# V's matmuls ahead of P's transposes in three of a unit's five slots

## The chip, the cores and the metric

The kernel runs on one core of one Trainium2 chip. The metric is device time in microseconds (us) of one execution; the times shown are medians of several runs. The engines are named as the profile names them: PE (TensorE's matmuls), PEld (its weight loads), DVE (VectorE), ACT (ScalarE), POOL (GpSimd) and SP (which issues the transfers).

## The reference

An attention with a learned bias, then a feed-forward layer whose gate is a cosine. In numpy, for q, k, v of 4 batches, 8 heads, 576 positions and 64 channels:

```
scores = q @ k.T / 8 + bias[head]          # bias from log positions through a small MLP
attn   = softmax(scores)                   # over the 576 keys
x      = (attn @ v) laid out as 2304 x 512 # tokens x model width
h      = x @ w_in                          # 512 -> 2048
out    = (h * cos(h)) @ w_out              # 2048 -> 512
```

## The kernel before

A first stage makes the bias table, a second the attention, a third the feed-forward layer. The change is in the second.

**Units and slots.** A unit is one pair of heads of one batch; there are 16 (`NU`), u = 0 to 15. A unit has five slots, j = 0 to 4, one for each block of queries: `tiles = [0, 1, 4, 2, 3]`, so the slots with j = 0, 1, 3, 4 have 128 queries of both heads, and j = 2 has the last 64 queries of both heads together. The text calls them first to fifth slot. The whole order of work is written by hand: `slot(i)` issues the instructions of slot i, and each engine runs its own instructions in exactly that order.

**What one slot issues on PE.** First the scores of this slot (`qk`, L416), 12 matmuls into two PSUM buffers (`ps_s`), one for each head; in the third slot 6. Then `halves` (L477, here called flips), which transposes by matmul the probabilities P of the block three slots earlier (`prev`) into two PSUM buffers `pm`, tags `m0` and `m1`, of which there is one each. Then `pv` (L545), V's matmuls, a part of the previous unit's output: `PV_EARLY` gives the first slot chunks 0 and 1 and the second slot chunks 2 to 4 of half 0, the fourth slot chunks 0 to 2 and the fifth chunks 3 and 4 of half 1; the third slot has none. A half sums up in one PSUM buffer (`ps_v`), of which there is one, so chunk 0 of a half has to wait until the half before has been copied away.

**The second slot** of units 1 to 13 already has `pv` ahead of `halves` (`v_first`); the copies of its flips are put off to the third slot (`held`). There, ahead of the scores, PE also transposes the q and k of unit u + 2 (`spare`).

**What the other engines issue.** In the order of each queue in a slot:

- DVE: for each head, scores plus bias and their extremum (L429), which also frees the head's score buffer; a copy of the flips in `m1` out of PSUM (`keep_main` with r = 1, L508); sums and reciprocals (L460, L463); in some slots one step that widens a weight (L101 to L107).
- ACT: the exponentials of the slot before, one for each head (`softmax_exp`, L447); a copy of the flips in `m0` (`keep_main` with r = 0, L505, tile PT); in the first and fourth slots a copy of leftover flips (`keep_left`, L505, tile PX), in the first also two of a q piece (L223); `keep_x` (L505, tile xT), which copies a finished half out of `ps_v`, in the third slot (half 0) and in the fifth (half 1). In the third slot, ACT has the exponentials, then the copy held over from the second slot, then a copy of q (L212, tile qt), then `keep_x`, then its own copy of the flips. In the fifth slot of odd units two weight operations stand in the queue: L93 ahead of the copy of the flips, L109 between it and `keep_x`.
- POOL: the splits of q and k (L185, L189) and the normalising of P (L470).

The copies of the flips fill PT, which `pv` reads later: the copies of a unit's flips of half 0 end in its fifth slot and are first read in the next unit's first slot; those of half 1 end in the third slot of the next unit and are first read in its fourth.

Of the kernel before, what the change touches and what calls it, by code (L numbers as in the profile page):

```python
# [28 lines left out]
def kernel(  # L29
# [44 lines left out]
    NU = len(units)  # L74
# [38 lines left out]
    with tc.manual_schedule():  # L113
# [248 lines left out]
        for n in range(len(todo) + 1):  # L362
            now = hts
# [172 lines left out]
        def pv(u, hf, chunks):  # L536
            hp, b = units[u]
            n = vN[u % 2]
            if 0 in chunks:
                X_[u, hf] = ps_v.tile([128, 512], F32, tag="v", name="pv")  # L540
            ps = X_[u, hf]
            for c in chunks:
                for h in range(2):
                    a, m = n[:, 4 * h + c if c < 4 else 8 + h], PT[u, hf][:, h, c, :] if c < 4 else PX[u, hf]
                    nc.tensor.matmul(  # L545
                        ps[64 * h : 64 * h + 64, 0 : WQ[hf]],
                        a,
                        m,
                        start=(c == 0),
                        stop=(c == 4),  # L550
                        tile_position=(0, 64 * h),
                        skip_group_check=True,
                    )
# [36 lines left out]
        def slot(i):  # L590
            u, j = divmod(i, 5)
            now, last, prev = get(i), get(i - 1), get(i - 3)
# [40 lines left out]
                behind = [(gone[0][:, 128 * n + 64 : 128 * n + 128], x) for n, x in enumerate(gone[1])]  # L633
            both = u + 2 if now and j == 0 and u and u + 2 < NU else None
            v_first = now and j == 1 and u and u + 2 < NU
            if v_first:
                for du, hf, chunks in PV_EARLY[j]:
                    pv(u + du, hf, chunks)
            pm = halves(prev, ahead, behind, both)
# [13 lines left out]
                shared["held"] = prev, pm  # L653
                prev = None
            for du, hf, chunks in PV_EARLY[j]:
                if 0 <= u + du < NU and not v_first:
                    pv(u + du, hf, chunks)
            if j == 2 and u >= 1:
                keep_x(u - 1, 0)
# [44 lines left out]
        for i in range(len(jobs)):  # L704
            slot(i)
# [152 lines left out]
        load_next()  # L858
        load_next()
        slot(len(jobs))  # L860
        ffn_step(0)
        slot(len(jobs) + 1)
        ffn1(steps[1])
        gate(steps[0])
# [64 lines left out]
```

## Time and profile before

| | |
|---|---|
| median of 3 runs | 702.76 us (701.63 to 705.5) |
| profiled execution | 705.26 us, span of its instructions 703.5 us |
| attention, units 2 to 13 | 14.30 us each |
| PE busy | 686.5 us, 98% of the span |
| DVE, ACT, POOL busy | 582.5, 434.9, 404.1 us (83%, 62%, 57%) |
| PE idle before scores L416, flips L477 into pm, V's matmuls L545 | 2.5, 0.1, 0.0 us |
| ACT idle before its copies of the flips (L505, PT) | 21.8 us |
| mean granted TensorE clock | 0.992 |

Busy is the time in which an engine works on an instruction; idle before a line is what its engine stood still just ahead of that line's instructions. In a timeline, each row gives a start in us from the span's start, the length, the engine, the line, what is written and read, and how many instructions are merged; an entry in brackets is idle time and who ended it. Instructions of one engine overlap a little, so what an instruction takes from its queue is the distance from its start to the next one's start.

### The profile page before, as it was taken

How to read it: one execution, taken by the hardware profiler on the slowest of the kernel's cores; microseconds unless marked ns; L12 is line 12 of the kernel's file. 1: busy time of each engine (PE TensorE's matmuls, PEld its weight loads, DVE VectorE, ACT ScalarE, POOL GpSimd, SP SyncE). 2: the span in 40 equal slices, each digit the busy share in tenths (PEclk: the TensorE clock that was granted, in tenths of full speed). 3: DMA queues.
4: the chain of work that ended last, by engine and by line, in shares of the span. 5: the costliest groups of instructions: out<-in, count | busy, mean ns of one | idle time of the engine just before them, and what ended most of it. 6: DMA issues, size and time to landing. Idle time of an engine off the chain costs nothing.

```text
span 703.5 us, 15609 instructions
## 1 busy us (share of the span) xinstructions
PE 686.5 (98%) x5747; PEld 563.1 (80%) x5747; DVE 582.5 (83%) x1340; ACT 434.9 (62%) x934; POOL 404.1 (57%) x486
## 2 busy tenths in 40 slices
PE   6988999999999999999999999999999999999997
PEld 3456777777777777789999889988889988899986
DVE  8978788888888888666897888999999998976656
ACT  5878789888888897646555564454544545433342
POOL 0204888989889889844555554464562653753300
PEclk9999899999999999999999999999999999999999
DMA  6787338436544611101102111111110100011112
GB/s 201 251 299 247 72 94 222 98 82 168 146 105 105 181 35 48 32 1 60 31 31 60 32 53 38 30 61 30 38 54 31 60 31 31 1 46 46 45 46 91
DMA packets 84445, 58.64 MB, mean 83 GB/s; under 512 B 62224, under 2 KB 70800, under 8 KB 84368
## 3 DMA queue, kind: packets, MB, share of 16 engines
q1 hardware_dynamic: 84080, 57.21, 28.1%
q8 instruction: 46, 0.75, 0.5%
q10 hardware_dynamic: 288, 0.43, 0.2%
q14 instruction: 31, 0.25, 0.1%
HBM read 42.00 MB, written 15.61 MB: 82 GB/s over the span
## 4 chain that ended last, share of the span: by engine, by line
PE 93%; DMA 2%; DVE 1%; SPq 1%; POOL 1%; issue 0%; ACT 0%; DVEq 0%; ACTq 0%; POOLq 0%
PE ph L731 29%; PE po L777 29%; PE pv L545 12%; PE s L416 11%; PE pm L477 6%; PE pa L328 5%; DMA sc<-rt 1%; PE pt L477 1%; PE spare L477 1%; DVE ht L313 1%; DMA pk<-in_pack_dram 1%; POOL P L470 0%; SPq L174 0%; ACT rt L346 0%; DMA nk<-in_k_dram 0%
## 5 line engine op out<-in xcount | busy, mean ns | idle before, releaser
L429 DVE CUSTOM_DVE_ANT_0 P<-s,bt 128x576 f32<-128x576 f32 x144 | 103.7, 753 | 24.7 <-PE s L416 24.7
L470 POOL TENSOR_SCALAR P<-P,rc 128x576 f32<-128x576 f32 x144 | 108.6, 766 | 25.2 <-DVE rc L463 10.9
L735 ACT ACTIVATE a<-ph,quarter 128x384 int32<-128x384 f32 x96 | 55.8, 581 | 100.7 <-PE ph L731 99.7
L531 POOL TENSOR_TENSOR xs<-xT,xs 128x384 fp32r<-128x384 f32 x96 | 107.5, 1119 | 8.0
L447 ACT ACTIVATE P<-P,m 128x576 f32<-128x576 f32 x144 | 110.0, 768 | 2.2 <-DVE m L429 2.1
L731 PE MATMUL ph<-xs,wpre 128*128 128x384 f32 x576 | 109.4, 338 | 0.0
L731 PE MATMUL ph<-xs,w 128*128 128x384 f32 x576 | 108.3, 337 | 0.0
L741 DVE SCALAR_TENSOR_TENSOR r<-a,ph 128x384 f32<-128x384 int32 x96 | 52.8, 550 | 65.0 <-ACT a L735 64.8
L731 PEld LDWEIGHTS ph<-xs,wpre 128*128 128x128 f32 x576 | 101.8, 188 | 5.4 <-DVE a L750 1.0
L731 PEld LDWEIGHTS ph<-xs,w 128*128 128x128 f32 x576 | 101.5, 188 | 4.8 <-DVE a L750 0.6
L746 ACT ACTIVATE r<-r,hpi 128x384 f32<-128x384 f32 x96 | 59.3, 617 | 73.8 <-DVE r L742 73.6
L416 PE MATMUL s<-kN,qT 64*128 64x288 f32 (+1 forms) x864 | 93.5, 315 | 2.5 <-DVE m L429 1.8
L416 PEld LDWEIGHTS s<-kN,qT 64*128 64x128 f32 (+1 forms) x864 | 72.1, 188 | 28.0 <-DVE dn L460 7.6
L530 POOL TENSOR_SCALAR xs<-xT 128x384 fp32r<-128x384 f32 x96 | 63.7, 663 | 38.3 <-PE ph L731 38.3
L545 PE MATMUL pv<-PT,vN 128*64 128x320 f32 (+1 forms) x512 | 77.0, 423 | 0.0
L760 DVE TENSOR_TENSOR gl<-a,gh 128x384 fp32r<-128x384 f32 x96 | 74.4, 776 | 1.7 <-ACT gh L754 1.7
L777 PE MATMUL po<-wpre,gh 128*128 128x512 f32 x288 | 75.3, 397 | 0.0
L777 PE MATMUL po<-w,gh 128*128 128x512 f32 x288 | 75.2, 395 | 0.0
L111 POOL TENSOR_TENSOR w<-wb,w 128x512 fp32r<-128x512 f32 x16 | 20.8, 1300 | 89.2 <-ACT w L109 89.2
L742 DVE SCALAR_TENSOR_TENSOR r<-a,r 128x384 f32<-128x384 int32 x96 | 61.4, 639 | 3.3
L754 ACT ACTIVATE gh<-a 128x384 fp32r<-128x384 f32 x96 | 49.8, 518 | 21.8 <-DVE a L750 21.8
L777 PEld LDWEIGHTS po<-wpre,gh 128*128 128x128 f32 x288 | 53.4, 188 | 9.4 <-issue 0.5
(97 smaller groups left out, 1176.4 us busy)
## 6 DMA issues: line engine op xcount, KB each, us to landing
sc<-rt SPq DMA_DIRECT2D x36, 295.5 KB, 3.5
raw<-in_moe_w_in_dram SPq DMA_DIRECT2D x16, 512.0 KB, 3.8
raw<-in_moe_w_out_dram SPq DMA_DIRECT2D x16, 512.0 KB, 3.5
bt<-sc SPq DMA_DIRECT2D x16, 288.0 KB, 3.4
out_dram<-acc SPq DMA_DIRECT2D x17, 256.0 KB, 2.0
nk<-in_k_dram SPq DMA_DIRECT2D x32, 128.0 KB, 3.4
nq<-in_q_dram SPq DMA_DIRECT2D x32, 128.0 KB, 3.1
bt<-sc SPq DMA_DIRECT2D x16, 256.0 KB, 3.9
```

Source lines behind the costliest of these rows:

```text
L416: nc.tensor.matmul(s[h][:, hf, 0:HALF], qTs[u % 2][r, a, 128 * t : 128 * t + 128] if t < 4 else qTs[u % 2][:, a, 512:640], kN[u][r, b, o : ...
L429: nc.vector.tensor_tensor_reduce(neg.rearrange("p (a x) -> p a x", a=2), s[h][:, :, 0:HALF], bias[hp, t, h].rearrange("p (a x) -> p a x", ...
L447: nc.scalar.activation(out=P[u, j][:, 576 * h : 576 * h + 576], in_=neg, func=AF.Exp, bias=m[:, 0:1], scale=-1.0, accum_out=dn[u, j][:, h ...
L470: nc.gpsimd.tensor_scalar(p, p, r, 1.0, ALU.mult, ALU.mult)
L530: nc.gpsimd.tensor_scalar(h, src, 1.0, 1.0, ALU.mult, ALU.mult)
L531: nc.gpsimd.tensor_tensor(l, src, f(h), ALU.subtract)
L545: nc.tensor.matmul(ps[64 * h : 64 * h + 64, 0 : WQ[hf]], a, m, start=(c == 0), stop=(c == 4), tile_position=(0, 64 * h), skip_group_check= ...
L731: nc.tensor.matmul(ps, a, x, start=(i == 0), stop=(i == 3 * KD - 1))
L742: nc.vector.scalar_tensor_tensor(r, n, -TWO_PI_LO, r, ALU.mult, ALU.add)
L746: nc.scalar.activation(out=r, in_=r, func=AF.Sin, scale=SIN_SCALE, bias=hpi)
L760: nc.vector.tensor_tensor(gl, a, f(G[key][0]), ALU.subtract)
L777: nc.tensor.matmul(O[n][i], a[:, 128 * i : 128 * i + 128], w, start=(i0 == 0 and p == 0), stop=(i0 == GF - 1 and p == 2),)
```

## The change

In units 1 to 15, the first, fourth and fifth slots issue `pv` directly behind `qk`, ahead of `halves`; in the last two units, where `v_first` is off, the second slot does too. Nothing is added or removed, and the queues of DVE, ACT, POOL and SP keep their order. The third slot is as it was. The copies of the flips are put off in the second slot of units 1 to 13 as before, and in no other.

```diff
             both = u + 2 if now and j == 0 and u and u + 2 < NU else None
             v_first = now and j == 1 and u and u + 2 < NU
-            if v_first:
+            v_ahead = v_first or (now and j != 2 and u)
+            if v_ahead:
                 for du, hf, chunks in PV_EARLY[j]:
                     pv(u + du, hf, chunks)
             pm = halves(prev, ahead, behind, both)
...
             for du, hf, chunks in PV_EARLY[j]:
-                if 0 <= u + du < NU and not v_first:
+                if 0 <= u + du < NU and not v_ahead:
                     pv(u + du, hf, chunks)
```

## Rows read from the trace of the kernel before

**Rows 1.** Windows of one unit each: length, busy time of the engines, clock.
```profile
211.70:226.00 14.30, 14.30 (x200) 10.64 (x198) 12.50 (x43) 11.75 (x32) 13.09 (x17) 1.00 0.45 116
226.00:240.30 14.30, 14.30 (x200) 10.64 (x198) 12.63 (x43) 12.84 (x34) 12.37 (x16) 1.00 0.80 212
```

**Rows 2.** Timeline of PE, first slot of unit 13 to its end.
```profile
245.74 1.06 PE L416 MATMUL s<-kN,qT 64*128 64x288 f32 x12
246.64 0.22 PE L477 MATMUL pm<-ident,nk 64*128 64x64 f32 x2
...
247.23 1.08 PE L545 MATMUL pv<-PT,vN 128*64 128x256 f32 x8
248.25 1.15 PE L416 MATMUL s<-kN,qT 64*128 64x288 f32 x12
249.32 1.08 PE L545 MATMUL pv<-PT,vN 128*64 128x256 f32 x8
...
252.90 0.65 PE L477 MATMUL pm<-ident,P 64*128 64x64 f32 x14
...
253.54 1.34 PE L416 MATMUL s<-kN,qT 64*128 64x288 f32 x12
254.60 0.78 PE L477 MATMUL pm<-ident,P 64*128 64x64 f32 x16
...
255.44 1.84 PE L545 MATMUL pv<-PT,vN 128*64 128x320 f32 x12
257.20 1.06 PE L416 MATMUL s<-kN,qT 64*128 64x288 f32 x12
258.10 0.59 PE L477 MATMUL pm<-ident,P 64*128 64x64 f32 x14
...
258.81 0.76 PE L545 MATMUL pv<-PT,vN 128*64 128x320 f32 x4
...
260.04 1.06 PE L416 MATMUL s<-kN,qT 64*128 64x288 f32 x12
```

**Rows 3.** Timeline of ACT in the same unit.
```profile
245.88 0.44 ACT L505 ACTIVATE xT<-pv 128x320 f32<-128x320 f32 x1 [0.67 <-PE pv L545]
...
247.74 0.37 ACT L505 ACTIVATE PT<-pm 128x256 f32<-128x256 f32 x1
...
248.57 0.39 ACT L505 ACTIVATE PX<-pt 128x256 f32<-128x256 f32 x1
248.85 0.77 ACT L447 ACTIVATE P<-P,m 128x576 f32<-128x576 f32 x1
...
251.89 0.58 ACT L505 ACTIVATE PT<-pm 128x512 f32<-128x512 f32 x1
252.87 0.60 ACT L212 ACTIVATE qt<-spare 128x512 f32<-128x512 f32 x1 [0.41 <-DVE kt L210]
...
253.77 0.60 ACT L505 ACTIVATE PT<-pm 128x512 f32<-128x512 f32 x1
...
255.42 0.60 ACT L505 ACTIVATE PT<-pm 128x512 f32<-128x512 f32 x1 [0.30 <-PE pm L477]
255.92 0.38 ACT L505 ACTIVATE PX<-pt 128x256 f32<-128x256 f32 x1
...
257.70 0.67 ACT L93 ACTIVATE wb<-raw 128x512 f32<-128x512 f32 x1
258.92 0.60 ACT L505 ACTIVATE PT<-pm 128x512 f32<-128x512 f32 x1 [0.55 <-PE pm L477]
259.42 0.62 ACT L109 ACTIVATE wpre<-wb 128x512 fp32r<-128x512 f32 x1
```

**Rows 4.** Timeline of DVE: the second head's scores of the first slot.
```profile
247.52 0.75 DVE L429 CUSTOM_DVE_ANT_0 P<-s,bt 128x576 f32<-128x576 f32 x1
```

**Rows 5.** Windows in units 0 and 1, columns as in rows 1.
```profile
67.00:71.00 4.00, 2.68 (x41) 2.02 (x37) 4.00 (x12) 2.80 (x8) 3.83 (x7) 1.00 0.43 95
71.00:75.00 4.00, 3.72 (x32) 3.18 (x33) 3.09 (x13) 2.81 (x11) 3.92 (x6) 0.52 0.71 161
```

## The prediction

> **What bounds the kernel now.** I read the page's busy table first: PE is busy for 98% of the span, so only PE's order and PE's waits count. Windows laid over single units then show the attention at a steady 14.30 us a unit with PE never idle, while ACT is busy for 11.75 us in one half of the windows and 12.84 in the other, DVE for 12.5 and POOL for 12.4 to 13.1 [rows 1]. So PE binds, but ACT has only 1.5 to 2.5 us a unit to spare. Every window runs at the full granted clock. Then the timelines of PE and ACT in one unit: what matters is how late ACT's copies of the flips start, because they stand in ACT's queue ahead of the next exponentials. In the fourth slot ACT waits 0.30 us for flips, in the fifth 0.55 [rows 3].
>
> **PE's own work: no gain, no loss.** The change adds no instruction and moves no transfer; it moves 28 matmuls of V and their weight loads past the flips in the first, fourth and fifth slots. Distances between starts of blocks [rows 2]: scores take 0.90 us ahead of flips (257.20 to 258.10), flips 0.71 ahead of V (258.10 to 258.81), 0.84 in the fourth slot and 0.59 in the first; V takes 1.23 (258.81 to 260.04), 1.76 in the fourth and 1.02 in the first. After the change three neighbourhoods count. Scores ahead of V: 1.07 in the second slot, but there the second head's scores come late, since DVE frees their buffer at 248.27, 0.02 after the scores began [rows 2, 4]; I take 1.00, between 0.90 and 1.07. Flips ahead of scores: 0.64 in the third slot; 0.65, and 0.54 for the first slot's shorter set. V ahead of flips I leave as it is. Scores behind flips stand only at 253.54, 1.06, with a wait inside; I take the same 1.00 ahead of V. Sums: fifth slot 0.90 + 0.71 + 1.23 = 2.84 becomes 1.00 + 1.23 + 0.65 = 2.88; first 2.51 becomes 2.56; fourth 1.06 + 0.84 + 1.76 = 3.66 becomes 1.06 + 0.10 + 1.76 + 0.65 = 3.57. Together nothing.
>
> **What it costs: ACT starts its copies later, and its queue becomes the bound.** The flips now end a slot on PE, later by V's 1.0 to 1.8 us, but ACT's queue keeps its order: copy of the flips, then the next exponentials. I follow the loop from the fourth slot's copy of one unit to that of the next. A copy starts 0.82 us after its flips began (258.10 to 258.92); behind V the flips go a little slower at first, so 0.87. The next scores start 0.65 after the flips began, 0.22 ahead of the copy.
>
> - Fourth slot's copy to fifth slot's. PE: -0.22 + 1.00 + 1.23 + 0.87 = 2.88. ACT: copy 0.50 (255.42 to 255.92), leftover copy and two exponentials 1.78 (to 257.70), 2.28 in all; in odd units one more operation of 0.67, 2.95 [rows 3]. The later counts: 2.88 in even units, 2.95 in odd ones.
> - Fifth slot's copy to the next first slot's. `keep_x` stands behind that copy, and V's chunk 0 in the first slot needs the buffer that it empties. ACT: 0.50, then `keep_x` 0.44 (245.88) and a handoff, 1.0; with the 0.62 of the weight copy between them 1.6. PE alone would be there at -0.22 + 1.00 = 0.78. So V waits 0.2, or 0.8 after odd units. Then V 1.01 and the first slot's flips until their copy, 0.75: 2.76 or 3.36.
> - First slot's copy to the end of the held copy. Here ACT runs without a wait: copy and q pieces 0.83 (247.74 to 248.57), leftover copy 0.28, four exponentials 3.04 (248.85 to 251.89), held copy 0.58: 4.73.
> - Held copy to the fourth slot's copy. The third slot's flips need the buffer that the held copy empties. Handoff 0.05, flips 0.64, scores 1.00, V 1.77, flips until their copy 0.87: 4.33. ACT's own work in between (copy of q, `keep_x`, the third slot's copy, one exponential) is short and ends first, so ACT stands still for about 2 us in the fourth slot, where it stood 0.30. V in the fourth slot needs the third slot's copy: 1.50 after the held one (252.87 to 253.77, and 0.60), against 1.69 on PE: covered by 0.2.
>
> Even units 2.88 + 2.76 + 4.73 + 4.33 = 14.70, odd units 2.95 + 3.36 + 4.73 + 4.33 = 15.37, mean 15.03 against 14.30: 0.73 a unit. DVE's queue has 1.8 us a unit to spare [rows 1] and takes up its later copies; POOL's normalising is needed later, not earlier, and costs nothing. If DVE's cover were gone, the second head's scores in the first slot would come late by some tenths, inside V's wait there.
>
> For units 2 to 15 that is 14 x 0.73 = 10.3 us. (The last two lack the held copy, but there V also moves ahead of the second slot's flips; I take the same price.) Unit 1 runs partly at the half clock and I give it nothing. Behind the last fifth slot, flips follow flips with no V between, so they wait for the copy: 0.87 + 0.50 + 0.10 against 0.65, 0.8 us. Sum 11.1. The feed-forward stage follows on a PE that has no gap, so nothing gives it back. The profiled execution's own 705.26 (703.5 of span, 1.8 around it) becomes 716.4; the median lies 2.5 under that execution, so 713.9, say 714.
>
> **Bounds.** With scores at 0.90 ahead of V and copies at 0.82, a unit costs 0.28 less: 4 us less in all, 710. With 1.07, handoffs of 0.15 and 0.10 more for scores behind flips, 0.4 more: 720.
>
> **Rivals.**
>
> *Faster: the order saves PE time and ACT keeps up.* From two V blocks, 12 matmuls in 1.76 us and 8 in 1.23 [rows 2]: 0.1325 each and 0.17 fixed, getting in and out. If the new neighbours made that free, 45 blocks (three a unit, 15 units) save 7.6 us: 695. The Trainium skill's page TensorEngine Tiling (Array Packing), section Tiling Modes, says that a change of tiling mode drains the engine; scores and flips both use half-height tiles, so by that rule scores behind flips need no drain, whereas scores behind V do. It also gives scores ahead of V a drain that scores ahead of flips lack, as the 1.07 beside 0.90 may show, so by the rule alone the count of drains a slot stays two. This rival decides only if ACT's loop is under 14.3, 0.7 shorter than I make it. Chance 5 in 100.
>
> *No change.* ACT's loop comes out at 14.3 because handoffs are shorter than I take them, or ACT's copies, started on a quieter bus, run shorter. Against it: 4.73 us of the loop is ACT alone, without a handoff from PE, and the legs are known to a tenth. Somewhere between 701 and 706. Chance 8.
>
> *The clock falls.* PE now has waits of 0.2 to 0.8 us. In unit 0 PE was busy 2.68 of 4 us, and in the next 4 us the granted clock was 0.52, the 1.2 GHz level, and PE did 32 matmuls where a unit at 2.4 GHz does 200 in 14.30, or 56 in 4 [rows 1, 5]. That loses 1.7 us of each 4; one such stretch a unit would add 24 us to the 11: 738. The Trainium skill's page TensorE: Matmul & The Clock Gate, section HAM oscillation, says that idle gaps between bursts of matmuls can bring the slow clock back. Against it: PE stays busy for 95% of a unit, and for some 80% of the worst slot. Chance 4.
>
> My forecast has the remaining 83, within its own range of 710 to 720.
>
> **Numbers.** About 0.5% (3.5 us) is what a measurement of this kernel can tell from no change. Faster by more than that: 0.05. Within it: the no-change case, 0.08. Slower: 0.87. The range reaches from 707, to take in part of the second rival, to 720.
>
> **What would show it.** Units of about 14.7 and 15.4 in turn, by the distance of the first slots' scores. ACT's wait for flips ahead of its fourth slot's copy near 2 us. Idle time of PE, now next to none, ahead of V in the first slot, ended by `keep_x` (L505, xT), longer behind odd units; and some 0.4 us ahead of the third slot's flips, ended by the held copy. Scores behind flips no longer than 1.00. The feed-forward stage unchanged. The prediction is wrong if ACT finishes its exponentials ahead of those copies, if V's first chunk never waits, or if the granted clock leaves 1.0 between 80 us and the end.

## The result: 1.4% slower

The changed kernel takes 713.29 us (median of 4 runs, 710.75 to 715.05) against 703.22 for the kernel before (701.63 to 705.5; a fourth run has joined the three behind the 702.76 above), a ratio of 1.0142 with a 95% interval from 1.0114 to 1.017: 10.1 us more. Forecast were 714.0, within 707 to 720, by a mechanism that the trace now has to bear out: ACT's queue takes the place of PE as what sets the length of a unit.

The spans of the two profiled executions, 703.5 and 709.0 us, differ by 5.5 only. The rest is at the start: in the execution after, unit 0 begins 1.9 us sooner (56.49 against 58.39 us), and unit 1 takes 15.04 us where the other's took 17.80, since the execution before has a stretch at the 1.2 GHz level from 71 us on [rows 5] and the one after has none. So the figure to compare is the stretch from unit 2's first scores to the first matmul of the feed-forward stage, in the PE timelines: 88.45 to 289.43 before, 200.98 us; 83.74 to 294.97 after, 211.23 us; 10.25 more. From there to the end of the span both take 414 us.

### The profile page after: what moved, and what is told of

Read it like the earlier page. It is cut to its first block, busy times and chain, and to the rows that moved or that the text cites. A ratio compares the mean times of both kernels' runs of the same rounds, so it can differ in the third digit from the quotient of the medians.

```text
span 709.0 us, 15612 instructions
## 1 busy us (share of the span) xinstructions
PE 680.5 (96%) x5747; PEld 556.8 (79%) x5747; DVE 584.3 (82%) x1340; ACT 432.2 (61%) x934; POOL 402.3 (57%) x486
## 4 chain that ended last, share of the span: by engine, by line
PE 77%; ACT 13%; issue 3%; DVE 3%; DMA 2%; POOL 1%; DVEq 0%; ACTq 0%; POOLq 0%
PE ph L732 29%; PE po L778 28%; PE pv L545 8%; ACT P L447 6%; PE pm L477 5%; PE pa L328 4%; PE s L416 3%; ACT PT L505 2%; DMA sc<-rt 1%; ACT PX L505 1%; ACT xT L505 1%; DVE ht L313 1%; ACT wpre L109 1%; ACT rt L346 1%; ACT qt L223 1%
## 5 line engine op out<-in xcount | busy, mean ns | idle before, releaser
L545 PE MATMUL pv<-PT,vN 128*64 128x320 f32 (+1 forms) x512 | 76.0, 418 | 4.7 <-ACT xT L505 4.3
L416 PEld LDWEIGHTS s<-kN,qT 64*128 64x128 f32 (+1 forms) x864 | 74.3, 186 | 7.2 <-DVE m L429 3.8
L477 PEld LDWEIGHTS pm<-ident,P 64*128 64x128 f32 x1184 | 47.2, 139 | 31.5 <-POOL P L470 8.8
L508 DVE COPY PT<-pm 128x512 f32<-128x512 f32 (+1 forms) x80 | 50.7, 634 | 25.4 <-PE pm L477 16.3
L505 ACT ACTIVATE PT<-pm 128x512 f32<-128x512 f32 (+1 forms) x80 | 44.1, 552 | 45.0 <-PE pm L477 35.1
```

What stands on the lines that cost most here:

```text
L416: nc.tensor.matmul(s[h][:, hf, 0:HALF], qTs[u % 2][r, a, 128 * t : 128 * t + 128] if t < 4 else qTs[u % 2][:, a, 512:640], kN[u][r, b, o : ...
L477: nc.tensor.transpose(out, i[p], ident[p, p], tile_position=(64 * r, 0))
L505: nc.scalar.activation(out=o, in_=i, func=AF.Copy)
L545: nc.tensor.matmul(ps[64 * h : 64 * h + 64, 0 : WQ[hf]], a, m, start=(c == 0), stop=(c == 4), tile_position=(0, 64 * h), skip_group_check= ...
```

## The profile after

Windows of units 6 and 7; columns as in [rows 1].

```profile
143.35:158.45 15.10, 14.21 (x199) 10.29 (x196) 12.61 (x46) 12.37 (x33) 12.32 (x17) 1.00 0.39 94
158.45:173.15 14.70, 14.08 (x201) 10.21 (x197) 12.79 (x41) 11.94 (x32) 12.97 (x18) 1.00 0.72 179
```

PE is no longer busy throughout: 0.89 and 0.62 us a unit are missing, where nothing was [rows 1]. The clock is 1.00 in both.

The chain of waits through an odd unit's fourth slot and on to the next even unit's fourth slot, with start and length; a chain lists what set the time, not what each engine did.

```profile
230.34 0.60 ACT PT L505
230.94 0.28 ACT PX L505
231.21 1.50 ACT P L447 x4
232.72 0.55 ACT wb L93
233.26 0.47 issue
233.74 0.62 ACT wpre L109
234.35 0.34 ACT xT L505
234.69 0.04 issue
234.73 1.08 PE pv L545 x8
...
236.43 0.39 ACT PT L505
...
238.99 1.71 ACT P L447 x5
240.70 0.49 ACT PT L505
241.19 0.14 issue
241.33 0.65 PE pm L477 x14
...
242.97 1.78 PE pv L545 x12
244.75 0.65 PE pm L477 x16
```

Before, 99% of this list between 88.5 and 283 us was PE. Now it is a loop: ACT from the late copy through the weight operations and `keep_x`, PE for V in the first slot, ACT through four exponentials to the held copy, PE through flips, scores, V and flips to the next late copy. 

The timeline of ACT in the same stretch answers to [rows 3].

```profile
230.34 0.60 ACT L505 ACTIVATE PT<-pm 128x512 f32<-128x512 f32 x1 [1.97 <-PE pm L477]
...
233.24 0.60 ACT L505 ACTIVATE PT<-pm 128x512 f32<-128x512 f32 x1
233.74 0.62 ACT L109 ACTIVATE wpre<-wb 128x512 fp32r<-128x512 f32 x1
234.25 0.43 ACT L505 ACTIVATE xT<-pv 128x320 f32<-128x320 f32 x1
...
236.43 0.39 ACT L505 ACTIVATE PT<-pm 128x256 f32<-128x256 f32 x1 [0.24 <-PE pt L477]
...
240.60 0.58 ACT L505 ACTIVATE PT<-pm 128x512 f32<-128x512 f32 x1
...
245.49 0.60 ACT L505 ACTIVATE PT<-pm 128x512 f32<-128x512 f32 x1 [1.97 <-PE pm L477]
```

The wait ahead of the fourth slot's copy is 1.97 us where it was 0.30 [rows 3]. The timeline of PE answers to [rows 2].

```profile
233.01 1.26 PE L416 MATMUL s<-kN,qT 64*128 64x288 f32 x12
234.73 1.08 PE L545 MATMUL pv<-PT,vN 128*64 128x256 f32 x8 [0.46 <-ACT xT L505]
...
239.84 1.06 PE L416 MATMUL s<-kN,qT 128*128 128x288 f32 x6
241.33 0.65 PE L477 MATMUL pm<-ident,P 64*128 64x64 f32 x14 [0.43 <-ACT PT L505]
...
242.92 1.83 PE L545 MATMUL pv<-PT,vN 128*64 128x320 f32 x12
244.69 0.71 PE L477 MATMUL pm<-ident,P 64*128 64x64 f32 x16
245.21 0.38 PE L416 MATMUL s<-kN,qT 64*128 64x288 f32 x1
...
246.30 0.76 PE L545 MATMUL pv<-PT,vN 128*64 128x320 f32 x4
...
249.38 1.08 PE L545 MATMUL pv<-PT,vN 128*64 128x256 f32 x8 [0.17 <-ACT xT L505]
...
255.97 0.65 PE L477 MATMUL pm<-ident,P 64*128 64x64 f32 x14 [0.44 <-ACT PT L505]
```

Both places of PE's waits are there: ahead of V in the first slot, 0.46 us behind an odd unit and 0.17 behind an even one, ended by `keep_x`; and ahead of the third slot's flips, 0.43 and 0.44, ended by the held copy. An idle entry counts only from the end of the matmul before, so distances say more: from the third slot's scores to its flips 1.49 us (239.84 to 241.33), 0.5 more than before (251.91 to 252.90), and from the first slot's scores to V 1.72 behind an odd unit (233.01 to 234.73) and 1.26 behind an even one (248.12 to 249.38), where 1.00 was taken without a wait. Nor do the waits add up to the cost of a unit: in unit 6 the first slot is 0.63 us longer than before and the third 0.38 (distances between the slots' first scores), but the fourth is 0.31 shorter (3.35 against 3.66).

## The experiments

The stretch named above, from unit 2's first scores to the feed-forward stage's first matmul, and the lengths of an even and an odd unit (6 and 7, distance between first slots' scores), come from the PE timelines, of one execution each; the ratio is the timed one against the kernel before.

| | ratio, 95% interval | stretch, us | units, us |
|---|---|---|---|
| before | | 200.98 | 14.30, 14.30 |
| changed | 1.0142 (1.0114 to 1.017) | 211.23 | 15.10, 14.70 |
| e1, fourth slot only | 1.0059 (1.0038 to 1.0079) | 205.25 | 14.73, 14.36 |
| e2, fifth slot only | 1.0053 (1.0032 to 1.0074) | 206.99 | 14.94, 14.42 |
| e3, first slot only | 1.0039 (1.0017 to 1.006) | 204.02 | 14.54, 14.53 |
| e4, fourth and fifth | 1.0064 (1.0042 to 1.0086) | 206.09 | 14.74, 14.40 |
| e5, `keep_x` first | 1.012 (1.0101 to 1.0139) | 206.55 | 14.67, 14.44 |
| e6, and exponentials earlier | 1.0089 (1.0065 to 1.0114) | 205.89 | 14.58, 14.43 |
| e7, changed, half exponentials | 1.0097 (1.0072 to 1.0122) | 208.13 | 14.86, 14.57 |
| e8, before, half exponentials | 0.9993 (0.9981 to 1.0005) | 200.90 | 14.29, 14.28 |
| e9, e6 and held copy earlier | 1.0056 (1.0035 to 1.0077) | 203.25 | 14.18, 14.41 |
| e10, e9, half exponentials | 1.0015 (0.9997 to 1.0033) | 202.55 | 14.18, 14.41 |

An even unit is long because the odd unit before it has the weight operations in its fifth slot, and the wait that they lengthen falls into the next unit's first slot.

The two columns do not rank the runs alike, because the ratio contains the start of the kernel, which varies (last section), and the stretch does not. The largest gap is at e5: its ratio is some 8.4 us, 1.5 less than that of the changed kernel, while its stretch is 5.6 over the kernel before. Three of its four runs had a mean granted clock of 0.995 (709.95 to 710.15 us) where ten of the thirteen runs of the kernel before beside it had 1.00; against the two of these with 0.994 and 0.995 (703.82 and 704.14) they are 6 us longer, as the stretch has it. Below, costs are taken from the stretch.

Three theories were put to the test. A: the order of ACT's queue, as in the prediction. B: PE itself is slower in the new order. C: DVE's copies of the other half of the flips, which start later too, are what PE waits for.

### e1 to e4: one or two of the moved slots

```diff
-            v_ahead = v_first or (now and j != 2 and u)
+            v_ahead = v_first or (now and j == 3 and u)        # e1
+            v_ahead = v_first or (now and j == 4 and u)        # e2
+            v_ahead = v_first or (now and j == 0 and u)        # e3
+            v_ahead = v_first or (now and j in (3, 4) and u)   # e4
```

> Only the fourth slot's V stands ahead of the flips. Theory A (ACT's queue): the fourth slot's copy waits some 2 us for its flips, the lateness runs through the queue, and PE waits ahead of V in the first slot behind odd units and ahead of the third slot's flips of the unit after. By the legs of the prediction with the fifth and first slot as before: units of about 14.55 and 14.9 us in turn, 6.5 us more in all (709.7). Rival B (PE itself is slower in the new order, each moved block by the same amount): a third of the 10.1 us of the whole change, 3.4 us (706.6), every unit 0.22 longer, no turn of odd and even.

> Only the fifth slot's V stands ahead of the flips. Theory A: the fifth slot's copy and keep_x behind it come late, above all in odd units, where two weight operations stand there too: units of about 14.3 and 14.9 in turn, 5.7 us more in all (708.9). Rival B: 3.4 us more (706.6), every unit 0.22 longer.

> Only the first slot's V stands ahead of the flips. Theory A: the copy of the first slot's flips and the four exponentials behind it come late, so the third slot's flips wait some 0.4 us for the held copy in every unit: units of 14.45, no turn of odd and even, 3.4 us more in all (706.6). Rival B: 3.4 us too (706.6), but with no wait of PE there.

> The fourth and the fifth slot's V stand ahead of the flips, the first slot's as before. Theory A: once the fourth slot has made ACT late, the fifth costs nothing on top: units of 14.55 and 14.9, 6.5 us more in all (709.7), the same as with the fourth slot alone, though each of the two alone costs about 6. Rival B: two thirds of the whole, 6.7 us, and the sum of what the two cost alone.

Windows of units 6 and 7, columns as before; first e1, then e3.

```profile
146.34:161.07 14.73, 14.10 (x197) 10.29 (x196) 12.46 (x45) 12.49 (x34) 12.21 (x17) 1.00 0.38 94
161.07:175.43 14.36, 14.36 (x196) 10.53 (x195) 12.46 (x42) 11.61 (x32) 12.90 (x18) 1.00 0.72 179
```

```profile
143.61:158.15 14.54, 14.20 (x197) 10.37 (x196) 12.77 (x43) 11.73 (x31) 12.36 (x17) 1.00 0.33 82
158.15:172.68 14.53, 14.18 (x196) 10.36 (x195) 12.84 (x43) 12.82 (x33) 13.05 (x18) 1.00 0.76 186
```

Odd and even differ with the fourth or the fifth slot moved, and not with the first alone, as A has it; in e1 PE is short of 0.63 us in unit 6 and of nothing in unit 7. What ended e1's wait needs a second look. Rows of e1 in unit 12: the third slot's flips, the held copy on ACT, and on POOL the normalising of the fifth slot's P, which these flips read, then that of the next P.

```profile
241.38 0.65 PE L477 MATMUL pm<-ident,P 64*128 64x64 f32 x14 [0.56 <-POOL P L470]
240.66 0.57 ACT L505 ACTIVATE PT<-pm 128x512 f32<-128x512 f32 x1
237.47 1.46 POOL L470 TENSOR_SCALAR P<-P,rc 128x576 f32<-128x576 f32 x2 [0.79 <-ACT qt L223]
...
240.58 1.47 POOL L470 TENSOR_SCALAR P<-P,rc 128x576 f32<-128x576 f32 x2
```

The profile names POOL (3.4 us over six even units), which would be a cause of its own. But the P that these flips read was done at 238.93, and the flips start 0.14 us after the held copy's end, as they do wherever PE waits there: 0.14 or 0.15 us in each of units 2 to 13 of the changed kernel and of e2 to e6, and in e1's even units. Where PE does not wait there, the copy ends 0.21 to 0.79 us ahead of them. So the held copy is what this wait is for in e1 too.

Over the stretch the fourth slot alone adds 4.3 us, the fifth alone 6.0, the first alone 3.0, and the fourth and fifth together 5.1, half of the sum of the two. Costs of PE's own order would add up, so B falls. The first slot's V is the other way round: in units 2 to 13 it costs 3.1 us alone, and 4.3 on top of the other two. None of these runs moves the second slot's V in the last two units, which the changed kernel does. A's sizes were near for the fifth and first slots (5.7 and 3.4 expected) and too high for the fourth alone and for the two together (6.5 expected for each). For e1 the trace shows where. Behind even units nothing is late: the held copy ends 0.44 us ahead of the flips, as in the kernel before (0.42), so these units have the 14.36 of PE's blocks and not 14.55. Behind odd units the loop took 14.70 (ACT's fourth-slot copies, 230.84 to 245.54), 0.2 less than 14.9.

### e5: `keep_x` ahead of the late copy

Against the changed kernel, in ACT's queue alone:

```diff
+            if v_ahead and j == 4:
+                keep_x(u - 1, 1)
             if prev:
                 keep_main(*prev, 0, pm[0])
             weights(i, W_MID)
-            if j == 4 and u >= 1:
+            if j == 4 and u >= 1 and not v_ahead:
                 keep_x(u - 1, 1)
```

> The changed kernel, but in the fifth slot ACT empties the buffer of V's sums (keep_x) ahead of its copy of the flips and ahead of the weight copy, not behind both. Theory A (ACT's queue sets the end, and keep_x behind a late copy is what V's chunk 0 waits for): the wait of 0.7 us ahead of V in the first slot goes, odd and even units no longer differ (15.1 and 14.7 become 14.7 both), 2.5 us less than the changed kernel: 710.8. The wait of 0.4 us ahead of the third slot's flips stays or grows. Rival C (DVE's copies of the other half of the flips, which also start later, are what PE waits for): no difference from the changed kernel, 713.3, and units still in turn.

Groups of PE's line L545 and of its line L477, with their idle time and what ended it; first of the changed kernel, then of e5.

```profile
L545 PE MATMUL pv<-PT,vN 128*64 128x320 f32 (+1 forms) x512 | 76.0, 418 | 4.7 <-ACT xT L505 4.3 <-DVE rc L463 0.3
L477 PE MATMUL pm<-ident,P 64*128 64x64 f32 x1184 | 56.8, 228 | 6.7 <-ACT PT L505 6.3 <-POOL qT L189 0.4
```

```profile
L477 PE MATMUL pm<-ident,P 64*128 64x64 f32 x1184 | 56.8, 228 | 6.8 <-ACT PT L505 6.4 <-POOL qT L189 0.4
...
L545 PE MATMUL pv<-PT,vN 128*64 128x320 f32 (+1 forms) x512 | 76.0, 418 | 0.3 <-DVE rc L463 0.3
```

The 4.3 us ahead of V are gone, the 6.3 ahead of the flips stand (6.4), and the stretch is 4.7 us shorter, more than the 2.5 expected, since the first slots behind even units gained too (unit 7: 14.70 to 14.44). Odd and even units still differ, which was not expected. DVE's queue was not touched: C falls, as far as this wait goes; e9 has the same for the other.

### e6: the fourth slot's exponentials in the gap

Against e5: the two exponentials of the fourth slot are issued in that slot, ahead of its copy, and no longer in the fifth.

```diff
-                if last:
+                if last and not (j == 4 and u):
                     for h in heads_of(last):
                         softmax_exp(*last, h)
...
+            if v_ahead and j == 3:
+                for h in heads_of((u, j)):
+                    softmax_exp(u, j, h)
             if v_ahead and j == 4:
                 keep_x(u - 1, 1)
```

> As the run before, and the fourth slot's own two exponentials are moved in ACT's queue from the fifth slot to ahead of the fourth slot's copy of the flips, into the 2 us in which ACT stands still there. Theory A: what is left is mostly the third slot's wait; units of 14.6 to 14.75, 4.7 us less than the changed kernel: 708.6, some 6 us above the kernel before. ACT's wait ahead of the fourth slot's copy falls from 2 us to some 0.5. Rival C: no difference, 713.3.

ACT's idle time ahead of its copies of the flips, over the whole kernel, first e5, then e6, and for e6 also ahead of `keep_x`.

```profile
L505 ACT ACTIVATE PT<-pm 128x512 f32<-128x512 f32 (+1 forms) x80 | 44.0, 550 | 41.4 <-PE pm L477 32.3 <-PE pt L477 8.7 <-ACT P L447 0.4
```

```profile
L505 ACT ACTIVATE PT<-pm 128x512 f32<-128x512 f32 (+1 forms) x80 | 43.9, 549 | 15.0 <-PE pm L477 9.7 <-PE pt L477 4.7 <-ACT P L447 0.4
L505 ACT ACTIVATE xT<-pv 128x256 f32<-128x256 f32 (+1 forms) x32 | 13.0, 407 | 16.3 <-PE pv L545 16.3
```

Ahead of these copies ACT stands still 26 us less, but most of that has only moved: 14 us of it now lie ahead of `keep_x` (16.3 against 2.0 in e5) and 7 ahead of exponentials that wait for DVE. In units 2 to 13 ACT stands still for 26.3 us in all, against 30.3 in e5, and the stretch is shorter by 0.7. The unit lengths came out a little under the expected 14.6 to 14.75, but nearly all of the gain was e5's. ACT's 2 us of standing still is where the lateness shows, not what it costs: as the prediction's legs have it, it is spent while PE works through the loop's last leg, and work put there does not shorten that leg.

### e7 and e8: exponentials over half of the columns

In both, ACT leaves out the other half of each exponential.

```diff
-                out=P[u, j][:, 576 * h : 576 * h + 576],
-                in_=neg,
+                out=P[u, j][:, 576 * h : 576 * h + 288],
+                in_=neg[:, 0:288],
```

> The changed kernel with each exponential over 288 of its 576 columns, so that the output is not the reference's: ACT has some 2.7 us a unit less to do. Theory A in its form that the order of ACT's queue matters: the wait ahead of the third slot's flips goes (four exponentials stand ahead of the held copy), the one ahead of V in the first slot stays (no exponential stands between the late copy and keep_x): units of 14.6 and 15.0 in turn, 3.2 us less, 710.1. In the form that ACT's load is what binds: both go, units of 14.3, 703.

> The kernel before with the same halved exponentials, output not the reference's. Theory A: PE binds there and ACT's lighter load changes nothing: units of 14.3, 702.7. If ACT had been part of the bound before, units would be shorter than 14.3.

PE's two lines again, in e7.

```profile
L477 PE MATMUL pm<-ident,P 64*128 64x64 f32 x1184 | 57.5, 228 | 1.3 <-ACT PT L505 1.0 <-POOL P L470 0.3
...
L545 PE MATMUL pv<-PT,vN 128*64 128x320 f32 (+1 forms) x512 | 76.0, 418 | 5.0 <-ACT xT L505 4.9
```

With 2.3 us less for ACT to do in unit 6 (busy 12.37 to 10.10), the wait for the held copy shrinks from 6.3 to 1.0 us, since four exponentials stand ahead of it; the wait for `keep_x`, which has none ahead of it behind the late copy, stays at 4.9. The units were to be 14.6 and 15.0 and are 14.57 and 14.86. So it is not ACT's load alone: its order costs as well. The kernel before does not move at all (14.29, ratio 0.9993): there PE binds.

### e9 and e10: the held copy between two exponentials

Against e6, in the third slot:

```diff
-                    for h in heads_of(last):
-                        softmax_exp(*last, h)
+                    softmax_exp(*last, 0)
                     keep_main(*held[0], 0, held[1][0])
+                    softmax_exp(*last, 1)
                     keep_pair(u + 2, "q", spare[:, :, 256:512])
```

e10 is e9 with the halved exponentials of e7.

> As e6, and in the third slot ACT's copy held over from the second slot stands between the two exponentials instead of behind both. Theory A: the wait of PE ahead of the third slot's flips, 0.5 us in each of 12 units in e6, goes; part of it comes back as a wait for the copy of q or for score buffers that DVE empties. Units of 14.3 to 14.4, 1.5 to 2.5 us less than e6, within 0.5% of the kernel before. If the third slot's wait were not due to the held copy's place behind the exponentials, units would stay at 14.45 and 14.57.

> As e9 with each exponential over 288 of its 576 columns, output not the reference's, so that ACT is far from full: this shows what PE (and DVE's emptying of the score buffers) make of the new order by themselves. By the sum of blocks of the prediction, which comes to nothing, 14.3 as before; by the rival in which the new neighbours on PE are cheaper, 14.1 or less; if the new order is dearer on PE, 14.5 and more, and the time stays above that of e8 by 3 us or more.

PE's lines in e9, then the windows of units 6 and 7 in e10 and in e8.

```profile
L477 PE MATMUL pm<-ident,P 64*128 64x64 f32 x1184 | 57.2, 228 | 0.8 <-ACT PT L505 0.8
...
L545 PE MATMUL pv<-PT,vN 128*64 128x320 f32 (+1 forms) x512 | 76.0, 418 | 0.3 <-DVE rc L463 0.3
```

```profile
141.77:155.95 14.18, 14.18 (x198) 10.24 (x195) 12.33 (x45) 10.50 (x32) 12.25 (x17) 1.00 0.39 98
155.95:170.36 14.41, 14.41 (x203) 10.45 (x199) 12.63 (x42) 10.66 (x33) 12.91 (x18) 1.00 0.68 170
```

```profile
142.03:156.32 14.29, 14.29 (x197) 10.64 (x195) 12.48 (x43) 9.93 (x31) 12.32 (x17) 1.00 0.34 83
156.32:170.60 14.28, 14.28 (x196) 10.62 (x194) 12.58 (x43) 11.01 (x33) 13.03 (x18) 1.00 0.68 176
```

The third slot's wait is gone (5.8 us in e6 to 0.8, what is left lies behind the last fifth slot), and units are 14.18 and 14.41, on average 14.30: the length before. With both waits of PE removed by three moves in ACT's queue, V ahead of the flips costs 0.3 us over units 2 to 13 together (171.89 against 171.59), most of it in unit 9 (14.59 where the other odd units take 14.41 to 14.44; the cause stays open), and gains nothing. e10 against e8 says the same with ACT lightly loaded: 14.30 and 14.29 on average. The other 2.0 of the 2.3 us that e9's stretch still has over the kernel before are in the last two units (14.19 against 13.66, and 17.17 against 15.72 from unit 15's first scores to the feed-forward stage), where PE's remaining waits were not looked into. With them the timed ratio, 1.0056, is just outside the 0.5% that was expected. No version here beats the kernel before.

## Why the prediction was right, point by point

**PE's own sum.** Forecast: together nothing. Shown by e10 against e8, and slot by slot: in e10's unit 6 the first, fourth and fifth slots take 2.45, 3.56 and 2.84 us (2.49, 3.55 and 2.96 in unit 7), where the sums had 2.56, 3.57 and 2.88. The parts were less exact: flips ahead of scores take 0.52 us in the fourth slot (244.69 to 245.21) where 0.65 was taken, because the first scores start between the last flips, and the scores are dearer in turn, 1.09 (245.21 to 246.30) where 1.00 was taken, so the sign "no longer than 1.00" missed. The Trainium skill's page TensorEngine Tiling (Array Packing), section Tiling Modes, has a change of tiling mode drain the engine; counted by it, a slot has two changes in either order. The units of e8 and e10, equal on average, agree with that count; the drain itself no run shows, and why e10's odd units are 0.23 us longer than its even ones stays open.

**The loop, leg by leg,** from the ACT timeline of the changed kernel, behind an odd unit's fourth slot:

| leg | forecast, us | measured, us |
|---|---|---|
| fourth slot's copy to the fifth's | 2.95 | 2.90 (230.34 to 233.24) |
| to the first slot's copy | 3.36 | 3.19 (to 236.43) |
| to the end of the held copy | 4.73 | 4.75 (to 241.18) |
| to the fourth slot's copy | 4.33 | 4.31 (to 245.49) |
| sum | 15.37 | 15.15 |

The second leg is the one that was off: the weight copy takes 0.51 us of ACT's queue (233.74 to 234.25), where its full length of 0.62 was taken, and the flips followed V a little sooner. That the last leg agrees to 0.02 us is in part luck: the third slot's flips start 0.15 us after the held copy's end (241.18 to 241.33) where a handoff of 0.05 was taken, and the fourth slot's flips need 0.80 us until their copy (244.69 to 245.49) where 0.87 was. The loop that starts in an even unit took 14.64 (245.49 to 260.13), where 14.70 was the forecast. The twelve units from 2 to 13 together took 179.1 us (83.74 to 262.83), 14.92 each: 0.62 over 14.30, where 0.73 was the forecast.

**The ends.** Behind the last fifth slot PE waited for the copy, as forecast:

```profile
293.21 0.53 PE L477 MATMUL pm<-ident,P 64*128 64x64 f32 x10 [0.78 <-ACT PT L505]
```

The idle entry of 0.78 us looks like the 0.8 that was forecast, but the forecast was of distances, and by these it is more: 1.62 us from the fifth slot's flips to these (291.59 to 293.21) against 0.65, so 0.97. Unit 14 cost 1.14 us (14.80 against 13.66) where 0.73 was taken, the price of the other units. So the shortfall of twelve units (0.11 x 12 = 1.3 us) was partly made up at the end, and 10.25 us stand against a sum of 11.1. That 714.0 lies only 0.7 us from 713.29 is partly luck too: the sum was 0.9 too high, and the median of the kernel before has risen by 0.5 with its fourth run.

**The rivals.** Faster: its junctions on PE were not cheaper (e10), and ACT did not keep up. No change: the loop takes 15.15 and 14.64 us in turn where PE's blocks take 14.30 (e10), and ACT's copies did not run shorter (0.60 us in the fourth slot before and after). The clock: 1.00 in every window of a unit shown here, where PE stays busy for 94% of the time or more, and over the whole profiled execution of the changed kernel, whose longest idle entry of PE from unit 2 to the feed-forward stage is 0.78 us. The page TensorE: Matmul & The Clock Gate of the Trainium skill, section HAM oscillation, speaks of idle gaps that bring the slow clock back. In these units no run shows it.

**What the prediction did not price** is each slot by itself: that the three do not add up (the expectation of e4 had this), and that the fourth slot, with the longest wait on ACT, is not the dearest: by itself it cost 4.3 us, the fifth 6.0.

## What to carry to other kernels

When one engine binds and another copies its results out, moving work ahead of the piece that is copied delays the copier by that work, and all that stands behind the copy in its queue; compare that delay with the copier's slack over a whole period, and follow the loop of copies and waits leg by leg from rows. The copier's own standing still is not the cost: remove each wait of the binding engine by its own cause (here `keep_x` behind a late copy, and a held copy behind four exponentials), and see what is left. Edits that share one late queue do not add up: two slots that cost 4.3 and 6.0 us alone cost 5.1 together, and a third that costs 3.1 alone cost 4.3 on top of them. And check a wait's named cause against distances: here the flips start 0.14 us after the held copy also where the profile names POOL.

## What the runs showed of the hardware

Scores that follow flips start ahead of the last flips' matmuls: in the fourth slot the first head's scores start at 245.21 and the last two flips from 245.24 on, so 18 flips take 0.52 us to the next block's start, where 0.65 was reckoned. These two flips read partitions 64 to 127 and the first head's scores 0 to 63, so on PE the order of starts is not quite the written order that the section on the kernel has for every engine.

The start of the kernel varies between executions by as much as an experiment here is worth: with a stretch of 6.8 us at the 1.2 GHz level in unit 1 (71.1 to 78.0 us), that unit takes 17.8 us, without it 14.8 to 15.2 in the traces of other versions. Beside the experiments, timed runs of the kernel before with a mean clock of 1.00 took 700.1 to 703.3 us, those with 0.990 to 0.995 took 702.1 to 705.8. That is why the spans of profiled executions don't rank these kernels, and the stretch from unit 2 on does.
